# One product of tile 1 ahead of the second half of the k weights, and the norm of tile 4 ahead of the first statistics of tile 5

## The chip, the cores and the metric

The kernel runs on one core of one Trainium2 chip. It is written against the engines directly: TensorE (PE, with its weight loads shown as PEld), VectorE (DVE), ScalarE (ACT), GpSimd (POOL) and SyncE (SP, which here issues most DMAs). Each engine works through its own list of instructions in order, and semaphores hold an instruction until what it needs is done on another engine. The metric is the time of one execution on the device in microseconds (us); less is better.

## The reference

Two branches are added to the input x (2048 rows of 640): linear attention with 32 heads on the layer-normed x, and a block that selects 8 rows by a score, runs a gated MLP on them and adds the result back to these rows.

```python
xn = _layernorm(x)                                   # over the 640 columns
qkv = (xn @ wqkv).reshape(B, S, 3, H, Dh)            # q, k, v of 32 heads, 20 wide
phi = lambda t: jnp.where(t > 0, t + 1, jnp.exp(t)) + 1e-6
kv = einsum("bhsd,bhse->bhde", phi(k), v);  z = einsum("bhsd->bhd", phi(k))
o = einsum("bhqd,bhde->bhqe", phi(q), kv) / (einsum("bhqd,bhd->bhq", phi(q), z)[..., None] + 1e-6)
A = o @ wo
r = x @ w_r;  idx = argsort(-r)[:8]
y = (silu(x[idx] @ w_gate) * (x[idx] @ w_up)) @ w_down * sigmoid(r[idx])
out = x + A + (x + scatter of y to the rows idx)
```

## The kernel before

The 2048 rows are 16 tiles of 128. In the first third of the time each tile t goes through these steps, which the change concerns:

- the rows of x are loaded by DMA (issued by SP) into the second half of `XX`;
- statistics of the two halves of a row, `ln_a` (L155) and `ln_b` (L158), and their aggregate `ln_g` (L161), all on DVE;
- the scale 1/sqrt(variance) in `SR`, by a logarithm and an exponential on ACT: `ln_r` (L164, L165);
- the norm, `ln_xn` (L169) on DVE: `XX` first half = (x - mean) * SR;
- the transpose into `xnT`. Tiles 0 to 3 do it on PE (`tr_mm`, L178, in two parts of 2 and 3 column blocks of 128) and are copied out of PSUM by ACT or DVE (`tr_cp`, L185, L187). Tiles from 4 on do it by a DMA transpose that SP issues (`tr_dma`, L190);
- the k projection, `K` (L214) on PE: five products (kc = 0 to 4, the blocks of 128 columns) for each half h of the k columns, each half into one PSUM bank. The weights `wk` come in two DMAs, half 0 issued by ACT and half 1 by SP; `wk`'s half 0 is 320 columns, half 1 has one more, the routing score. `KA` is kc 0 and 1, `KB` is kc 2 to 4;
- phi(k): an exponential `PHe` (L233) and a relu `PHr` (L236) on ACT for each half, then `PHb` (L252) on DVE, which puts the tile's phi(k) into `pk`;
- `G` (L261, L268) on PE: the tile's normed rows times `pk`, summed over all tiles in PSUM banks 0 to 5.

After the last tile the matrix G, whose product with the v weights is the kv of the reference, is used for the rest: q projections (L489), denominators, the output matrix, the MLP of the chosen rows, and the output tiles (L761). The change does not touch these.

The order of every engine's work is written out by hand: the kernel is under a manual schedule, so the order of the calls in the text is the order on each engine, and waits are put where data demand them. Tiles 0 to 3 are interleaved call by call (L347 to L448); tiles 4 to 15 run in a loop (L449 to L479), where tile t's `K` stands ahead of `G(t - 1)`, `PHb(t - 1)` goes ahead of the norm of tile t + 2, and the statistics run three and four tiles ahead. PSUM banks 6 and 7 hold `K` of tiles 0, 2, 3 and up, banks 4 and 5 `K` of tile 1; banks 0 and 1 serve the PE transposes of tiles 0 and 2, banks 2 and 3 those of tiles 1 and 3, until `G` takes banks 0 to 5.

Around the first edit the PE order is: K(0) half 0; K(1) half 0, kc 0 and 1; K(0) half 1, kc 0 and 1; K(1) half 1, kc 0 and 1; K(0) half 1, the rest; transposes of tile 2 (2 blocks); K(1) half 1, the rest; transposes of tile 2 (3 blocks); K(1) half 0, the rest; K(2). The third and later blocks of tile 1 reach `xnT` by the copy `tr_cp(1, 1, 2, act)`. Around the second edit the DVE order is: `PHb(1)`, `ln_a(5)`, `ln_xn(4)`, `ln_b(5)`, `PHb(2)`, `ln_g(5)`, `ln_xn(5)`, `ln_a(6)`, `ln_b(6)`, `ln_g(6)`, `PHb(3)`.

Of the kernel before, what the change touches and what calls it, by code (L numbers as in the profile page):

```python
# [38 lines left out]
def kernel(  # L39
# [109 lines left out]
    def st_of(t):  # L149
        if t not in sts:  # L150
            sts[t] = tmp.tile([P, 2, nc.vector.BN_STATS_DIM], F32, tag="stats", name="stats", bufs=4)
        return sts[t]

    def ln_a(t):
        dve.bn_stats(out=st_of(t)[:, 0, :], in_=XX[:, t, 1, 0:320])  # L155
# [4 lines left out]
    def ln_g(t):  # L160
        dve.bn_aggr(out=MV[:, t, :], in_=sts[t][:])  # L161

    def ln_r(t):
        act.activation(lnv[:, t : t + 1], MV[:, t, 1:2], AF.Ln, bias=eps5[:])  # L164
        act.activation(SR[:, t : t + 1], lnv[:, t : t + 1], AF.Exp, scale=-0.5)  # L165

    def ln_xn(t, parts=((0, D),)):
        for a, b in parts:
            dve.tensor_scalar(out=XX[:, t, 0, a:b], in0=XX[:, t, 1, a:b], scalar1=MVf[:, t, 0:1],  # L169
                              scalar2=SR[:, t : t + 1], op0=ALU.subtract, op1=ALU.mult)  # L170
# [9 lines left out]
    def tr_cp(t, h, b0, eng):  # L180
        k0, k1 = TRP[h]
        src = PS[:, b0 + h, :].bitcast(BF16)[:, 0 : (k1 - k0) * P].rearrange("p (k c) -> p k c", c=P)
        dst = xnT[:, k0:k1, t * P : (t + 1) * P]
        if eng is act:
            act.copy(dst, src)  # L185
        else:
            dve.tensor_copy(dst, src)  # L187
# [17 lines left out]
    def off(t, h):  # L205
        return T - 1 - t if t != 1 and h else 0

    def K(t, hs=(0, 1), b=6, ks=range(KC)):
        for h in hs:
            if t > 4:  # L210
                pad(1)
            w = HW + h
            for kc in ks:
                pe.matmul(  # L214
                    PS[:, b + h, off(t, h) : off(t, h) + w],
                    lhsT=xnT[:, kc, t * P : (t + 1) * P],
                    rhs=wkh[h][:, kc, 0:w],
                    start=(kc == 0),
                    stop=(kc == KC - 1),
                )  # L220
# [3 lines left out]
    def phi_src(t, h, b):  # L224
        return PS[:, b + h, off(t, h) : off(t, h) + HW]

    def er(t):
        if t not in phis:
            phis[t] = tuple(tmp.tile([P, D], BF16, tag=k, name=k, bufs=3) for k in ("ek", "rk"))
        return phis[t]  # L230

    def PHe(t, h, b=6):
        act.activation(er(t)[0][:, h * HW : (h + 1) * HW], phi_src(t, h, b), AF.Exp)  # L233
# [20 lines left out]
    def pad(n):  # L254
        for _ in range(n):
            pe.ldweights(zero[:, 0:P])  # L256

    def G(t, ks=range(KC)):
        for a in ks:
            lhsT = XX[:, t, 0, a * P : (a + 1) * P]  # L260
            pe.matmul(  # L261
                PS[:, a, :], lhsT=lhsT, rhs=pk[:, t, 0:512],
                start=(t == 0), stop=(t == T - 1),
            )
            if t > 4:
                pad(2)
            if a < 4:
                pe.matmul(  # L268
                    PS[:, 5, a * P : (a + 1) * P], lhsT=lhsT, rhs=pk[:, t, 512:D],
                    start=(t == 0 and a == 0), stop=(t == T - 1), skip_group_check=True,  # L270
                )
# [74 lines left out]
    KA, KB = (range(0, 2), range(2, KC))  # L346
# [24 lines left out]
    tr_cp(1, 1, 2, act)  # L371
    ln_g(2)
    K(1, (0,), 4, KA)
    ln_r(2)
    K(0, (1,), 6, KA)
    PHe(0, 0, 6)
# [9 lines left out]
    tr_mm(2, 1, 0)  # L386
    ones(2)
    tr_cp(2, 0, 0, act)
    K(1, (0,), 4, KB)
    ln_g(3)  # L390
    PHr(0, 1, 6)
    tr_cp(2, 1, 0, dve)
# [30 lines left out]
    G(0, (3,))  # L423
    ln_r(4)
    K(3, (1,), 6, KB)
    ln_a(5)
    K(3, (0,), 6, KA)
    ln_xn(4)
    PHe(3, 1, 6)
    G(1)  # L430
    PHr(3, 1, 6)
# [531 lines left out]
```

## Time and profile before

| | |
|---|---|
| time, median of 3 runs | 106.49 us (106.16 to 106.72) |
| time of the profiled execution | 106.39 us |
| its span, first to last instruction | 104.7 us |
| granted TensorE clock, share of full speed | 0.999 |
| PE, DVE, ACT busy | 96%, 79%, 66% of the span |
| HBM read, written | 13.80 MB, 3.65 MB |

The span is what the profile shows between the first and the last instruction of the program; the time holds 1.7 us more around it. Times in the views are microseconds from the start of the span unless marked ns. Engines are named PE, PEld, DVE, ACT, POOL and SP; a q behind the name marks the sequencer that issues. L214 is line 214 of the kernel before. A matmul's end is modelled, so a busy PE is read by the distance of the starts of its products rather than by its share.

### The profile page before, as it was taken

How to read it: one execution, taken by the hardware profiler on the slowest of the kernel's cores; microseconds unless marked ns; L12 is line 12 of the kernel's file. 1: busy time of each engine (PE TensorE's matmuls, PEld its weight loads, DVE VectorE, ACT ScalarE, POOL GpSimd, SP SyncE). 2: the span in 40 equal slices, each digit the busy share in tenths (PEclk: the TensorE clock that was granted, in tenths of full speed). 3: DMA queues.
4: the chain of work that ended last, by engine and by line, in shares of the span. 5: the costliest groups of instructions: out<-in, count | busy, mean ns of one | idle time of the engine just before them, and what ended most of it. 6: DMA issues, size and time to landing. Idle time of an engine off the chain costs nothing.

```text
span 104.7 us, 2781 instructions
## 1 busy us (share of the span) xinstructions
PE 100.8 (96%) x924; PEld 72.8 (70%) x1148; DVE 82.8 (79%) x187; ACT 68.9 (66%) x171; POOL 16.3 (16%) x60
## 2 busy tenths in 40 slices
PE   6999999999999999999999999999999999999980
PEld 3357666668888888888777777875566767777760
DVE  1778989998888897873787867878988997888870
ACT  4288956766666666888599999886993997000000
POOL 7800000530000000000000025270000500000230
PEclk9999999999999999999999999999999999999999
DMA  2999914334756655899998999911460136895344
GB/s 57 299 347 379 282 38 87 74 66 86 146 134 80 152 122 125 179 267 346 241 391 275 343 332 377 348 51 39 160 228 9 30 101 202 192 364 185 130 129 125
DMA packets 23024, 19.67 MB, mean 188 GB/s; under 512 B 10594, under 2 KB 21474, under 8 KB 23010
## 3 DMA queue, kind: packets, MB, share of 16 engines
q1 hardware_dynamic: 21880, 19.01, 62.2%
q10 hardware_dynamic: 842, 0.46, 1.6%
q8 instruction: 8, 0.13, 0.6%
q0 software_dynamic: 288, 0.01, 0.3%
q14 instruction: 6, 0.05, 0.2%
HBM read 13.80 MB, written 3.65 MB: 167 GB/s over the span
## 4 chain that ended last, share of the span: by engine, by line
PE 89%; DMA 5%; SPq 1%; issue 1%; DVE 1%; DVEq 0%
PE PS L489 21%; PE PS L214 20%; PE PS L761 20%; PE PS L261 17%; DMA wk<-in_A_wqkv_dram 5%; PE PS L268 3%; PE PS L713 2%; PE PS L673 1%; SPq L103 1%; PE PS L555 1%; PE PS L737 1%; PE PS L684 1%; PE PS L282 1%; DVE o L774 1%; PE PS L635 1%
## 5 line engine op out<-in xcount | busy, mean ns | idle before, releaser
L214 PE MATMUL PS<-wk,xnT 128*128 128x320 bf16 (+1 forms) x160 | 25.0, 300 | 0.1
L261 PE MATMUL PS<-pk,XX 128*128 128x512 bf16 x80 | 23.7, 379 | 0.0
L489 PE MATMUL PS<-xnT,wq 128*128 128x512 bf16 x100 | 22.4, 379 | 0.0
L761 PE MATMUL PS<-Mb,pqT 128*128 128x320 bf16 (+4 forms) x165 | 22.1, 295 | 0.0
L256 PEld LDWEIGHTS <-zero 128*128 128x128 bf16 x224 | 18.2, 97 | 5.5
L233 ACT ACTIVATE ek<-PS 128x320 bf16<-128x320 f32 x32 | 14.0, 437 | 7.9 <-PE PS L214 7.9
L761 PEld LDWEIGHTS <-pqT 128*128 128x128 bf16 x165 | 15.8, 97 | 4.7 <-issue 0.3
L214 PEld LDWEIGHTS <-xnT 128*128 128x128 bf16 x160 | 15.2, 97 | 4.8 <-issue 0.3
L252 DVE SCALAR_TENSOR_TENSOR pk<-ek,rk 128x640 bf16<-128x640 bf16 x16 | 13.1, 817 | 4.1 <-ACT rk L236 3.9
L546 DVE SCALAR_TENSOR_TENSOR pqT<-qe,qr 128x512 bf16<-128x512 bf16 x20 | 13.6, 685 | 3.0 <-ACT qr L498 2.9
L497 ACT ACTIVATE qe<-PS 128x512 bf16<-128x512 f32 x20 | 12.3, 615 | 3.2 <-PE PS L489 3.2
L268 PE MATMUL PS<-pk,XX 128*128 128x128 bf16 x64 | 14.0, 219 | 0.0
L236 ACT ACTIVATE rk<-PS 128x320 bf16<-128x320 f32 x32 | 14.0, 436 | 0.0
L489 PEld LDWEIGHTS <-wq 128*128 128x128 bf16 x100 | 11.6, 118 | 2.9 <-issue 0.2
L498 ACT ACTIVATE qr<-PS 128x512 bf16<-128x512 f32 x20 | 12.3, 614 | 0.0
L770 DVE TENSOR_TENSOR o<-PS,XX 128x640 bf16<-128x640 f32 x11 | 9.0, 822 | 2.9 <-PE PS L761 2.0
L261 PEld LDWEIGHTS <-XX 128*128 128x128 bf16 x80 | 7.8, 98 | 4.2
L202 ACT ACTIVATE XX<-XX,MR,SR 128x640 bf16<-128x640 bf16 x11 | 9.4, 912 | 0.0
L155 DVE BATCH_NORM_STATS2 stats<-XX 128x6 f32<-128x320 bf16 x16 | 7.4, 463 | 1.9 <-DMA XX<-in_A_x_dram 1.9
L169 DVE TENSOR_SCALAR XX<-XX,MVf,SR 128x640 bf16<-128x640 bf16 (+2 forms) x17 | 7.3, 437 | 1.3 <-ACT SR L165 1.3
L158 DVE BATCH_NORM_STATS2 stats<-XX 128x6 f32<-128x320 bf16 x16 | 7.7, 479 | 0.0
L274 POOL MEMSET XX<- 128x1 bf16 x18 | 1.9, 112 | 35.2 <-DMA xnT<-XX 21.0
(114 smaller groups left out, 101.2 us busy)
## 6 DMA issues: line engine op xcount, KB each, us to landing
out_dram<-o SPq DMA_DIRECT2D x15, 160.0 KB, 2.0
XX<-in_A_x_dram SPq DMA_DIRECT2D x3, 640.0 KB, 7.9
wg<-in_B_w_gate_dram SPq DMA_DIRECT2D x5, 384.0 KB, 8.8
wu<-in_B_w_up_dram SPq DMA_DIRECT2D x5, 384.0 KB, 6.1
wd<-in_B_w_down_dram SPq DMA_DIRECT2D x1, 1920.0 KB, 11.3
wv<-in_A_wqkv_dram SPq DMA_DIRECT2D x5, 160.0 KB, 3.5
wq<-in_A_wqkv_dram SPq DMA_DIRECT2D x1, 800.0 KB, 6.2
hi_d<-XX SPq DMA_DIRECT2D x1, 800.0 KB, 3.9
```

What stands on the lines that cost most here:

```text
L214: pe.matmul(PS[:, b + h, off(t, h) : off(t, h) + w], lhsT=xnT[:, kc, t * P : (t + 1) * P], rhs=wkh[h][:, kc, 0:w], start=(kc == 0), stop=( ...
L233: act.activation(er(t)[0][:, h * HW : (h + 1) * HW], phi_src(t, h, b), AF.Exp)
L236: act.activation(er(t)[1][:, h * HW : (h + 1) * HW], phi_src(t, h, b), AF.Relu)
L252: dve.scalar_tensor_tensor(out=pk[:, t, :], in0=ek[:], scalar=1.0, in1=rk[:], op0=ALU.min, op1=ALU.add)
L256: pe.ldweights(zero[:, 0:P])
L261: pe.matmul(PS[:, a, :], lhsT=lhsT, rhs=pk[:, t, 0:512], start=(t == 0), stop=(t == T - 1),)
L268: pe.matmul(PS[:, 5, a * P : (a + 1) * P], lhsT=lhsT, rhs=pk[:, t, 512:D], start=(t == 0 and a == 0), stop=(t == T - 1), skip_group_check= ...
L489: pe.matmul(PS[:, bank, :], lhsT=by5(wq[:, kc, :])[:, m, :], rhs=xnT[:, kc, tb * TBLK : (tb + 1) * TBLK], start=(kc == 0), stop=(kc == KC ...
L497: act.activation(e, PS[:, bank, :], AF.Exp)
L498: act.activation(r, PS[:, bank, :], AF.Relu)
L546: dve.scalar_tensor_tensor(out=pqT[:, m, tb * TBLK : (tb + 1) * TBLK], in0=e, scalar=1.0, in1=r, op0=ALU.min, op1=ALU.add,)
L761: pe.matmul(PS[:, b, o : o + c1 - c0], lhsT=pqT[:, kc, t * P : (t + 1) * P], rhs=Mb[:, kc, c0:c1], start=(kc == 0), stop=(kc == KC - 1))
```

## The change

Two calls change their place. Of the three products that `K(1, (0,), 4, KB)` issued in one go (kc 2, 3, 4 of tile 1 against half 0 of the k weights), the one for kc = 2 now stands right behind the products for kc 0 and 1, ahead of the first product on half 1 of the weights; kc 3 and 4 stay where they were. And on DVE the norm of tile 4 now stands ahead of the first statistics of tile 5. No instruction is added or removed.

```diff
     ln_g(2)
     K(1, (0,), 4, KA)
+    K(1, (0,), 4, (2,))
     ln_r(2)
     K(0, (1,), 6, KA)
     PHe(0, 0, 6)
...
     tr_cp(2, 0, 0, act)
-    K(1, (0,), 4, KB)
+    K(1, (0,), 4, (3, 4))
     ln_g(3)
...
     G(0, (3,))
     ln_r(4)
     K(3, (1,), 6, KB)
-    ln_a(5)
     K(3, (0,), 6, KA)
     ln_xn(4)
+    ln_a(5)
     PHe(3, 1, 6)
     G(1)
```

## The prediction

> **What bounds the kernel now.** I read the page first, then the chain of waits, then busy time by stage.
>
> ```profile
> span 104.7 us, 2781 instructions
> PE 100.8 (96%) x924; PEld 72.8 (70%) x1148; DVE 82.8 (79%) x187; ACT 68.9 (66%) x171; POOL 16.3 (16%) x60
> ...
> PE 89%; DMA 5%; SPq 1%; issue 1%; DVE 1%; DVEq 0%
> ```
> ```profile
> 2.20 5.50 DMA wk<-in_A_wqkv_dram
> ```
> ```profile
> 8.90:13.45 4.55, 4.55 (x41) 3.15 (x39) 4.37 (x12) 4.49 (x16) 0.20 (x2) 1.00 1.03 296
> ```
> ```profile
> 7.75:101.00 93.25, 93.25 (x891) 69.14 (x1115) 77.31 (x168) 64.65 (x160) 11.89 (x41) 1.00 0.65 186
> ```
>
> The chain runs through the DMA of the second half of the k weights (issued 2.20, landed 2.20 + 5.50 = 7.70) and from there almost wholly through TensorE (its 89%). In the two rows by stage the columns are stretch, its length, busy PE, PEld, DVE, ACT, POOL, granted clock, DMA share and GB/s. PE fills all of the 93.25 from 7.75 to 101 at a clock of 1.00. So nothing after 7.75 can soak up lost PE time: what PE loses there, the end loses, and what it gains has to be let through by every later wait. ACT is as full as PE from 8.90 to 13.45 (4.49 of 4.55), where the change lies; DVE is nearly so. The change moves hundredths of a microsecond, so the waits must be read one by one.
>
> **Part 1, the moved product.** Rows of the timeline, each from a narrow window of its own and put in order of time: start, length, engine, line, operation; a row with a count is a run of equal instructions, and brackets tell how long the engine stood before it and for whom.
>
> ```profile
> 6.35 0.15 PEld L214 LDWEIGHTS <-xnT 128*128 128x128 bf16 x2
> 6.41 0.30 PE L214 MATMUL PS<-wk,xnT 128*128 128x320 bf16 x1
> 7.04 0.48 ACT L185 COPY xnT<-PS 128x384 bf16<-128x384 bf16 x1
> 7.12 0.57 PE L214 MATMUL PS<-wk,xnT 128*128 128x320 bf16 x3
> 7.75 0.10 PEld L214 LDWEIGHTS <-xnT 128*128 128x128 bf16 x1 [0.26 <-issue]
> 9.24 0.37 ACT L185 COPY xnT<-PS 128x256 bf16<-128x256 bf16 x1
> 9.53 0.43 PE L214 MATMUL PS<-wk,xnT 128*128 128x320 bf16 x2
> 9.66 0.10 PEld L214 LDWEIGHTS <-xnT 128*128 128x128 bf16 x1
> 11.48 0.47 DVE L158 BATCH_NORM_STATS2 stats<-XX 128x6 f32<-128x320 bf16 x1
> 11.87 0.27 DVE L187 COPY xnT<-PS 128x256 bf16<-128x256 bf16 x1
> 11.98 0.59 PE L261 MATMUL PS<-pk,XX 128*128 128x512 bf16 x2
> ```
>
> The pace of these products is (0.57 - 0.30) / 2 = 0.135 us. The last one ahead of the weights starts at 7.12 + 2 x 0.135 = 7.39, so the next could start at 7.525; it starts at 7.75. That hole of 0.225 takes the moved product, if its own operand is there: columns 2 to 4 of tile 1, copied by ACT until 7.04 + 0.48 = 7.52. A wait hands over in about 0.04 (ACT's end at 15.83 to DVE's start at 15.87, rows in part 2), so its weights load from 7.56. From the start of a load to its product is 6.41 - 6.35 = 0.06: product at 7.62, next at 7.62 + 0.135 = 7.755 against 7.75. The row does not show this load behind a wait followed by one more load, so I bound the lag by 0.06 and by the load's full 0.10: the next product is 0.005 to 0.045 late; I take 0.01, since the 0.06 is a row of the same line. [...]
>
> What is removed is one of the three products of tile 1 that end at 9.53 + 2 x 0.135 = 9.80, thus 0.135. It is not all let through. The first load of tile 2 waits for the copy that ends at 9.24 + 0.37 = 9.61; with the handover that is 9.65, and it stands at 9.66 now. So the load cannot move; its product, at 9.80 now, can start at 9.65 + 0.06 = 9.71, a gain of 0.09. Next, G of tile 0 into bank 2 needs the copy of tile 3 out of that bank: 11.87 + 0.27 = 12.14, handed over by 12.18. In the row of two products the second ends at 11.98 + 0.59 = 12.57 and lasts 0.38 (the 512-wide ones), so it starts at 12.19 now. And that copy stands on DVE right behind the second statistics of tile 4 (11.48 + 0.40 = 11.88), so an earlier PE does not pull it forward. Of 0.135 there is 0.01 to 0.02 left after 12.2. Bounds: -0.135 (all kept) to nothing; I take -0.01, since both waits have rows. ACT is not moved either, being full up to 13.45 and started off by the products on the second half; it only shares their 0.01.
>
> **Part 2, the norm of tile 4 ahead of the first statistics of tile 5.** Rows of DVE, with those of ACT and PE that they meet, chosen in the same way:
>
> ```profile
> 12.46 0.81 DVE L252 SCALAR_TENSOR_TENSOR pk<-ek,rk 128x640 bf16<-128x640 bf16 x1
> 13.19 0.49 DVE L155 BATCH_NORM_STATS2 stats<-XX 128x6 f32<-128x320 bf16 x1
> 13.25 0.20 ACT L165 ACTIVATE SR<-lnv 128x1 f32<-128x1 f32 x1
> 13.59 0.43 DVE L169 TENSOR_SCALAR XX<-XX,MVf,SR 128x640 bf16<-128x640 bf16 x1
> 13.94 0.48 DVE L158 BATCH_NORM_STATS2 stats<-XX 128x6 f32<-128x320 bf16 x1
> 14.34 0.80 DVE L252 SCALAR_TENSOR_TENSOR pk<-ek,rk 128x640 bf16<-128x640 bf16 x1
> 15.07 0.20 DVE L161 BATCH_NORM_AGGREGATE MVf<-stats 128x2 bf16<-128x12 f32 x1
> 15.41 0.38 PE L261 MATMUL PS<-pk,XX 128*128 128x512 bf16 x1
> 15.63 0.20 ACT L165 ACTIVATE SR<-lnv 128x1 f32<-128x1 f32 x1
> 15.87 0.45 DVE L169 TENSOR_SCALAR XX<-XX,MVf,SR 128x640 bf16<-128x640 bf16 x1 [0.60 <-ACT SR L165]
> 16.23 0.49 DVE L155 BATCH_NORM_STATS2 stats<-XX 128x6 f32<-128x320 bf16 x1
> 16.69 0.12 PEld L214 LDWEIGHTS <-xnT 128*128 128x128 bf16 x2 [0.15 <-DMA xnT<-XX]
> 17.27 0.77 DVE L252 SCALAR_TENSOR_TENSOR pk<-ek,rk 128x640 bf16<-128x640 bf16 x1
> 18.09 0.38 PE L261 MATMUL PS<-pk,XX 128*128 128x512 bf16 x1
> ```
>
> The norm needs the scale that ACT finishes at 13.25 + 0.20 = 13.45. In the old order the statistics of tile 5 run from 13.19 and cover that wait; the norm follows at 13.59. In the new order DVE is free for the norm at 13.19 and must stand until 13.45 + 0.04 = 13.49 (the same handover: 15.83 to 15.87). The norm, and with it the transpose DMA of tile 4, gains 0.10; everything behind it on DVE pays. The statistics follow a norm by 0.36 (15.87 to 16.23), so they start at 13.85; the second statistics by 0.40 (13.19 to 13.59), at 14.25 against 13.94; pk of tile 2 at 14.65 against 14.34. All of that is 0.31 late.
>
> First customer: G of tile 2 at 15.41 needs pk of tile 2. That ended at 14.34 + 0.80 = 15.14; now 15.45, handed over at 15.49: PE stands 0.08. This also uses up the 0.01 of part 1. Second customer: the aggregate of tile 5 (15.07 to 15.38), its two ACT steps, its norm. In the old trace DVE waits 0.60 there for ACT, but that wait is a round trip that starts from the aggregate, so it hides nothing: the norm goes from 15.87 to 16.18, the statistics of tile 6 from 16.23 to 16.54, pk of tile 3 from 17.27 to 17.58, its end from 18.04 to 18.35. Third customer: G of tile 3 stands at 18.09, which is 0.05 behind the end of pk of tile 3; it has no slack. It goes to 18.40, 0.31 late. The 0.08 from G of tile 2 lies inside this and is not added. The earlier transpose of tile 4 is worth nothing: its product at 16.69 waits for it by a hair now, but PE arrives there 0.08 later anyway.
>
> From there PE and DVE are both 0.31 late, side by side, and no later stretch has room.
>
> **The transposes behind it.** SP issues the one of tile 5 when the norm of tile 5 ends, 0.31 later:
>
> ```profile
> 16.34 1.58 SPq L190 DMA_TRANSPOSE xnT<-XX  x1
> 19.22 0.27 PEld L214 LDWEIGHTS <-xnT 128*128 128x128 bf16 x2
> 22.07 0.11 PEld L214 LDWEIGHTS <-xnT 128*128 128x128 bf16 x2
> ```
> ```profile
> DMA to landing us min/median/max: 2.6/2.7/3.3
> ```
> ```profile
> DMA to landing us min/median/max: 2.7/2.7/2.7
> ```
> ```profile
> DMA to landing us min/median/max: 3.2/3.2/3.2
> ```
>
> The three landing rows are from the view of the transposes' line (L190): nine of them together, tile 5 alone, tile 6 alone. Issued at 16.65 and landed 2.7 later that is 19.35; the load that waits for it stood at 19.22 and would come at 19.53. Covered by 0.14 (after the handover). If it took the 3.2 of tile 6 it would land at 19.85 and cost 19.89 - 19.53 = 0.36 more. Between 2.6 and 3.3 I take its own 2.7, cost nothing. Tile 6 (load at 22.07) shifts with PE.
>
> **Sum**, against the profiled execution's own 106.39 (span 104.7): 0.01 late at the weights, which ACT and then DVE carry along, + 0.31 at G of tile 3; the 0.01 left of the product is lost in the stand at G of tile 2. 106.39 + 0.32 = 106.71. The median of the runs is 106.49, 0.10 above that execution; on it the sum would be 106.81. I forecast 106.75, between them, +0.25% on the median.
>
> **The rivals.** (a) Not slower, the head start kept because DVE's hole never reaches PE: what is in favour is a real hole of 0.225 and a transpose that PE waits for at 16.69. It needs pk of tile 3 to end by 18.05, thus a DVE delay of zero, thus the scale of tile 4 ready by 13.15 in place of 13.45. Against it: ACT is full up to there. Then the gain lies between 0.01 and 0.135: 106.26 to 106.38, on the median 106.36 to 106.48. (b) Clearly slower: the transpose of tile 5 lands late. For it: one of its neighbours took 3.2, and it decides from 2.84 us on (19.53 - 0.04 - 16.65). Against it: tile 5 took 2.7 itself, and the median of nine is 2.7. Price 0.32 + 0.36: 107.07, on the median 107.17. (c) The moved product doesn't fit into the hole. Where the weights land at 7.5 or before, it stands in front of the work on them: without it that work starts at 7.53, with it at 7.755, and ACT and DVE go along, 0.22 late. The price is then 0.32 + 0.22 = 0.54: 106.93. For it: the landing is the only thing here that no engine sets. Against it: in this execution the weights landed 0.18 behind the copy, at 7.70. (d) The change doesn't do what it says, because DVE's order makes no difference to G of tile 3: then part 1 alone is left, 106.38, the weak end of (a), whose chance it shares.
>
> **How the numbers follow.** Forecast 0.58, (a) with (d) 0.14, (b) 0.20, (c) 0.08. The range takes in the low end of (a), 106.26, and (b) on the median, 107.17, to within 0.02: 106.25 to 107.15, with the forecast's own between 106.55 and 106.95. By 0.5% (0.53 us, about what a measurement of this kernel can tell from no change): slower gets all of (b) and half of (c), whose 0.54 lies on the bound, and 0.07 of the forecast, for terms mis-sized by 0.2: 0.31. Faster gets half of (a), 0.07: even its full 0.135 is a quarter of the bound, so this is room for a gain that no row shows. The same: the rest, 0.62.
>
> **What would show it.** In the changed kernel: a product at about 7.6 in the hole, the first product on the second half still at 7.75 to 7.80; a hole of about 0.3 on DVE ahead of the norm of tile 4, released by ACT; pk of tile 2 and 3 ending near 15.45 and 18.35; PE standing some 0.08 ahead of G of tile 2 and 0.2 ahead of G of tile 3. Wrong would be: no hole on DVE there, or G of tile 3 at or before 18.1, or the loads of tile 5 released by the DMA.

## The result, and the profile after

The changed kernel takes 106.88 us (median of 22 runs, 106.65 to 107.47), the kernel before 106.56 in the same comparison. The ratio is 1.0035, with a 95% interval of 1.0020 to 1.0051: slower by about a third of a percent, inside the half percent that was called no change, and 0.13 above the forecast of 106.75. The difference of the two medians is 0.32.

The page of the changed kernel:

```profile
span 105.0 us, 2773 instructions
PE 100.0 (95%) x916; PEld 72.5 (69%) x1148; DVE 82.6 (79%) x187; ACT 68.8 (66%) x171; POOL 16.3 (16%) x60
...
PE 89%; DVE 3%; DMA 2%; issue 1%; DVEq 0%
```

Eight of PE's 924 products have no record here (the change removes none), so a single gap of 0.22 on PE with no releaser is a missing row and not a wait. The span is 0.3 longer. The DMA of the k weights, 5% of the chain before, is gone from the chain. That is the first thing to look at: why? The timeline around the moved product, chosen rows, and then the row of the half-1 load in the table of DMA issues (the last number is the time from issue to landing), of the kernel before and of the changed one:

```profile
6.66 0.90 ACT L185 COPY xnT<-PS 128x256 bf16<-128x256 bf16 x2
7.61 0.11 PEld L214 LDWEIGHTS <-xnT 128*128 128x128 bf16 x2 [0.22 <-ACT xnT L185]
7.62 0.45 PE L214 MATMUL PS<-wk,xnT 128*128 128x320 bf16 x2
```
```profile
wk<-in_A_wqkv_dram SPq DMA_DIRECT2D x1, 400.0 KB, 5.5
```
```profile
wk<-in_A_wqkv_dram SPq DMA_DIRECT2D x1, 400.0 KB, 5.3
```

In this execution the weights landed at 2.20 + 5.3 = 7.50, before the copy that the moved product waits for was done (6.66 + 0.90 = 7.56). The product starts at 7.62, and the first product on half 1, the second of that row, at 7.76. Without the moved product it could have started at 7.56, one pace of 0.135 behind the product at 7.42. So the hole of 0.225 that the trace of before showed was not there, and the moved product made one of its own, 0.06 of standing for the copy.

The second part, in the order in which it unrolls (chosen rows):

```profile
12.42 0.82 DVE L252 SCALAR_TENSOR_TENSOR pk<-ek,rk 128x640 bf16<-128x640 bf16 x1
13.26 0.20 ACT L165 ACTIVATE SR<-lnv 128x1 f32<-128x1 f32 x1
13.49 0.45 DVE L169 TENSOR_SCALAR XX<-XX,MVf,SR 128x640 bf16<-128x640 bf16 x1 [0.26 <-ACT SR L165]
13.86 0.49 DVE L155 BATCH_NORM_STATS2 stats<-XX 128x6 f32<-128x320 bf16 x1
13.97 1.20 SPq L190 DMA_TRANSPOSE xnT<-XX  x1
14.65 0.81 DVE L252 SCALAR_TENSOR_TENSOR pk<-ek,rk 128x640 bf16<-128x640 bf16 x1
15.52 0.38 PE L261 MATMUL PS<-pk,XX 128*128 128x512 bf16 x1
16.18 0.45 DVE L169 TENSOR_SCALAR XX<-XX,MVf,SR 128x640 bf16<-128x640 bf16 x1 [0.60 <-ACT SR L165]
16.66 1.48 SPq L190 DMA_TRANSPOSE xnT<-XX  x1
16.85 0.30 PE L214 MATMUL PS<-wk,xnT 128*128 128x320 bf16 x1
17.58 0.77 DVE L252 SCALAR_TENSOR_TENSOR pk<-ek,rk 128x640 bf16<-128x640 bf16 x1
18.41 0.38 PE L261 MATMUL PS<-pk,XX 128*128 128x512 bf16 x1
19.53 0.27 PEld L214 LDWEIGHTS <-xnT 128*128 128x128 bf16 x2
```

The bracket behind the norm at 13.49 is the new hole on DVE, released by ACT's scale. From it all of DVE runs late: pk of tile 2 by 0.31 (14.34 to 14.65), the norm of tile 5 by 0.31, pk of tile 3 by 0.31 (17.27 to 17.58). PE pays at G of tile 3: 18.09 before, 18.41 now. The transpose of tile 4 is issued 0.08 earlier (14.05 to 13.97), which brings nothing: PE reaches that tile's products at 16.85, 0.14 later than before.

### The profile page after: what moved, and what is told of

The parts are those of the page before. It is cut to its first block, busy times and chain, and to the rows that moved or that the text cites. A ratio compares the mean times of both kernels' runs of the same rounds, so it can differ in the third digit from the quotient of the medians.

```text
span 105.0 us, 2773 instructions
## 1 busy us (share of the span) xinstructions
PE 100.0 (95%) x916; PEld 72.5 (69%) x1148; DVE 82.6 (79%) x187; ACT 68.8 (66%) x171; POOL 16.3 (16%) x60
## 4 chain that ended last, share of the span: by engine, by line
PE 89%; DVE 3%; DMA 2%; issue 1%; DVEq 0%
PE PS L214 21%; PE PS L490 21%; PE PS L762 20%; PE PS L261 16%; PE PS L268 4%; DMA XX<-in_A_x_dram 2%; PE PS L714 2%; PE PS L674 1%; PE PS L556 1%; PE PS L178 1%; PE PS L738 1%; PE PS L685 1%; PE PS L282 1%; DVE stats L155 1%; DVE XX L169 1%
## 5 line engine op out<-in xcount | busy, mean ns | idle before, releaser
L261 PE MATMUL PS<-pk,XX 128*128 128x512 bf16 x75 | 22.7, 379 | 0.0
```

The lines of the kernel that those rows point to most:

```text
L261: pe.matmul(PS[:, a, :], lhsT=lhsT, rhs=pk[:, t, 0:512], start=(t == 0), stop=(t == T - 1),)
```

## The experiments

Each kernel was timed against the kernel before on the same chip; kernels sent together share its runs. The number to follow in the traces is the distance from the first product on half 1 of the k weights to the first product of G of tile 3. It leaves out what happens ahead of the first point, which differs from execution to execution. "Rest" is the profiled execution's time less the first point. Both starts are read from the timeline.

| kernel | half 1 (or its first part) landed | first product on it | G of tile 3 | distance | profiled time | rest |
|---|---|---|---|---|---|---|
| before | 7.71 | 7.75 | 18.09 | 10.34 | 106.39 | 98.64 |
| changed | 7.50 | 7.76 | 18.41 | 10.65 | 106.76 | 99.00 |
| changed, again | 7.44 | 8.08 | 18.73 | 10.65 | 107.02 | 98.94 |
| product alone | 7.19 | 7.71 | 18.04 | 10.33 | 106.34 | 98.63 |
| norm alone | 7.21 | 7.50 | 18.17 | 10.67 | 106.53 | 99.03 |
| norm alone, again | 7.79 | 7.92 | 18.56 | 10.64 | 106.88 | 98.96 |
| changed, hole filled | 7.88 | 7.92 | 18.24 | 10.32 | 106.54 | 98.62 |
| norm, hole filled | 7.73 | 8.00 | 18.38 | 10.38 | 106.72 | 98.72 |
| DVE delayed | 7.67 | 7.71 | 18.42 | 10.71 | 106.83 | 99.12 |
| split load | 6.66 | 7.52 | 17.88 | 10.36 | 106.47 | 98.95 |
| split, product | 6.62 | 7.87 | 18.20 | 10.33 | 106.77 | 98.90 |
| split, norm | 6.71 | 7.47 | 18.11 | 10.64 | 106.69 | 99.22 |
| split, both | 6.56 | 7.81 | 18.46 | 10.65 | 107.03 | 99.22 |
| split, x loads merged | 6.31 | 7.59 | 17.96 | 10.37 | 106.26 | 98.67 |

**The moved product alone.**

```diff
     K(1, (0,), 4, KA)
+    K(1, (0,), 4, (2,))
...
-    K(1, (0,), 4, KB)
+    K(1, (0,), 4, (3, 4))
```

> The moved product alone, DVE's order as before. My theory: the product's 0.135 us is not let through; G of tile 0 into bank 2 still starts at about 12.2 and G of tile 3 at about 18.1, so the ratio to the kernel before lies between 1.000 (weights of half 1 landing at 7.7, where the product fits into the hole) and 1.002 (weights landing at 7.5, where it stands ahead of their work). Rival, the head start is kept: G of tile 3 at about 17.95, ratio 0.9987.

106.65 us, ratio 1.0007 (0.9991 to 1.0024). The first product of G of tile 3:

```profile
18.04 0.38 PE L261 MATMUL PS<-pk,XX 128*128 128x512 bf16 x1
```

That is 10.33 behind the first product on half 1, against 10.34: of the 0.135 taken out of the later work at most 0.01 is left, as the two waits of the prediction had it. The weights had landed at 7.19 here and their work still started only at 7.71, for PE first stood for the copy that the moved product needs, and then did that product:

```profile
7.56 0.11 PEld L214 LDWEIGHTS <-xnT 128*128 128x128 bf16 x2 [0.22 <-ACT xnT L185]
```

**The norm's move alone**, twice.

```diff
-    ln_a(5)
     K(3, (0,), 6, KA)
     ln_xn(4)
+    ln_a(5)
```

> The norm of tile 4 ahead of the first statistics of tile 5, alone. My theory: DVE stands about 0.3 us ahead of the norm, pk of tile 3 ends 0.31 later, G of tile 3 starts at about 18.4; ratio 1.003. Rival, the order on DVE is free and the difference comes from the moved product: ratio 1.000, G of tile 3 at about 18.1. Rival, the earlier transpose of tile 4 pays: ratio 0.999.

> The norm's move alone, once more, since its first time (0.12 us above the kernel before) fell short of the 0.31 that its trace showed and of the 0.35 that it cost beside the split load. My theory: the first time was drawn from executions whose weights landed early; now 0.25 to 0.35 above, ratio 1.002 to 1.0035. Rival, without the moved product about two thirds of it are taken back: 0.12 again, ratio 1.001.

First time 106.65 us, ratio 1.0007 (0.9990 to 1.0024); second time 106.67, ratio 1.0012 (0.9990 to 1.0033). The traces show the expected wait and the expected distance in both (10.67 and 10.64); the rows of the first:

```profile
13.25 0.45 DVE L169 TENSOR_SCALAR XX<-XX,MVf,SR 128x640 bf16<-128x640 bf16 x1 [0.20 <-ACT SR L165]
```
```profile
18.17 0.38 PE L261 MATMUL PS<-pk,XX 128*128 128x512 bf16 x1
```

The time agrees less well: 0.31 us would be a ratio of 1.0029, which is inside the second interval and outside the first. The repeated expectation was missed. See the open point below.

**The hole filled, by an earlier scale.** In the changed kernel, ACT does the scale of tile 4 ahead of the relu of tile 2's half 0, and the two products of tile 3 that write that relu's bank go behind G of tile 1, so that they don't wait for it.

```diff
+    ln_r(4)
     PHr(2, 0, 6)
     G(0, (3,))
-    ln_r(4)
     K(3, (1,), 6, KB)
-    K(3, (0,), 6, KA)
     ln_xn(4)
     ln_a(5)
     PHe(3, 1, 6)
     G(1)
+    K(3, (0,), 6, KA)
```

> The changed kernel, with the scale of tile 4 brought up on ACT ahead of the relu of tile 2's half 0, and the two products that reuse that bank moved behind G of tile 1. My theory, it is the lateness of ACT's scale that makes DVE stand: the scale is ready at about 13.13, DVE has no hole ahead of the norm, pk of tile 3 ends at about 18.05 and G of tile 3 starts at about 18.1; ratio to the kernel before 1.000 to 1.002 (what the moved product costs at the weights). Rival, having the statistics behind the norm is itself what costs (the order, not the wait): G of tile 3 stays at about 18.4, ratio 1.003 or more.

106.55 us, ratio 0.9996 (0.9981 to 1.0012). ACT's scale, DVE's norm and G of tile 3:

```profile
13.09 0.20 ACT L165 ACTIVATE SR<-lnv 128x1 f32<-128x1 f32 x1
```
```profile
13.33 0.45 DVE L169 TENSOR_SCALAR XX<-XX,MVf,SR 128x640 bf16<-128x640 bf16 x1
```
```profile
18.24 0.38 PE L261 MATMUL PS<-pk,XX 128*128 128x512 bf16 x1
```

The norm still stands ahead of the statistics, but its bracket is gone: the scale ends at 13.29, and the norm starts at 13.33, as soon as pk of tile 1 lets it. G of tile 3 comes 10.32 behind the first product on half 1. With the order of the change on DVE and without the wait the 0.31 are gone; it was the wait and not that order. (This kernel also moves two products on PE, so it is not a test of the wait by itself; the delayed DVE below tests it from the other side.)

**The same without the moved product.** The diff is the last one on top of the norm's move alone.

> The norm's move with the scale of tile 4 brought up on ACT and the two products behind G of tile 1, without the moved product. My theory: DVE has no hole ahead of the norm, G of tile 3 follows the first product on half 1 by 10.3 as in the kernel before, in place of 10.66; ratio 0.999 to 1.001, thus 0.3 faster than the norm's move alone. Rival, the order costs without the wait: 1.003.

106.72 us, ratio 1.0013 (0.9993 to 1.0033). The distance is 10.38, as in the kernel before, against 10.64 of the norm's move on the same chip. In the time it is not faster than that move (106.67). So the trace bears out the expectation, and the timed runs miss it: 0.3 faster was expected.

**DVE delayed, with the old order.**

```diff
     ln_xn(4)
+    dve.memset(spare[:], 0.0)
     PHe(3, 1, 6)
```

> The kernel before, order unchanged, with a memset of 128x640 (about 0.3 us on DVE) behind the norm of tile 4, so that the transpose of tile 4 keeps its time and only pk of tile 2, the norm of tile 5 and pk of tile 3 come later. My theory: G of tile 3 has no slack and starts about 0.3 later, at 18.4; ratio 1.003, as in the changed kernel. Rival, the loss comes through another road than DVE's lateness: G of tile 3 at about 18.1, ratio 1.000.

106.84 us, ratio 1.0027 (1.0005 to 1.0048). The memset, and G of tile 3 (line numbers are one higher in this kernel, for the line that makes `spare`):

```profile
14.08 0.33 DVE L430 MEMSET spare<- 128x320 uint32 x1
```
```profile
18.42 0.38 PE L262 MATMUL PS<-pk,XX 128*128 128x512 bf16 x1
```

The distance is 10.71, the rest 99.12. Lateness of DVE behind the norm of tile 4, put in by itself, costs about what the change costs and at the same place: 0.37 in the distance, for a memset of 0.33. No later stretch takes it back in this trace.

**The load of half 1 split**, so that the weights of blocks 0 and 1 are always there in time, and on top of it the product, the norm's move and both.

```diff
-    ld(sp, wkh[1][:, :, 0:HW], wqkv_v[:, :, D + HW : 2 * D])
+    ld(sp, wkh[1][:, 0:2, 0:HW], wqkv_v[:, 0:2, D + HW : 2 * D])
+    ld(sp, wkh[1][:, 2:KC, 0:HW], wqkv_v[:, 2:KC, D + HW : 2 * D])
```

> The kernel before with the load of the second half of the k weights cut in two (blocks 0 and 1, then 2 to 4), so that the first products on it no longer wait for the whole. In the profiles so far that load landed between 7.19 and 7.88, and the first product on it started at the later of about 7.53 and the landing. My theory: it now starts at about 7.53 always; G of tile 3 follows 10.34 behind it, at about 17.87; the time loses its spread and ratio is 0.998 to 0.999. Rival, the extra issue on SP delays the loads of x behind it and eats this: ratio 1.000 or more.

> The split load and the moved product. My theory: with the weights always there, the product only stands in front of their work: first product on half 1 at about 7.72 in place of 7.53, later distance to G of tile 3 shorter by 0.05 (10.29); 0.10 to 0.15 us slower than the split load alone. Rival, the product is free or helps even so: equal to the split load alone, or faster by 0.1.

> The split load and the norm of tile 4 ahead of the first statistics of tile 5. My theory: G of tile 3 follows the first product on half 1 by 10.66 in place of 10.34; 0.32 us slower than the split load alone. Rival, as the time of the norm alone hinted (0.12 above the kernel before): a part of it is taken back behind G of tile 3, so 0.1 slower than the split load alone.

> The split load and both parts of the change. My theory: first product on half 1 at about 7.72, G of tile 3 at about 18.38; 0.45 to 0.5 us slower than the split load alone, the sum of the two. Rival, the two parts cover each other: slower than the split load alone by no more than the norm's part.

| | time | ratio to before |
|---|---|---|
| split | 106.63 | 1.0018 (1.0001 to 1.0035) |
| split, product | 106.67 | 1.0022 (1.0004 to 1.0040) |
| split, norm | 106.98 | 1.0059 (1.0036 to 1.0082) |
| split, both | 107.07 | 1.0067 (1.0044 to 1.0090) |

On this common ground the norm's move costs 106.98 - 106.63 = 0.35 and both parts 0.44. The product costs 0.04 to 0.09 by the medians, less than the 0.10 to 0.15 expected, and its distance is 10.33, not the 10.29 expected. The traces show more than the medians: the first product on half 1 starts at 7.87 and 7.81 with it, 7.52 and 7.47 without it, though the weights had landed by 6.71 in all four. Of that, 0.15 lies ahead of the change, since the first k product, too, starts at 6.54 and 6.50 with it, 6.39 and 6.35 without it. From the first k product on it is 1.33 and 1.31 against 1.13 and 1.12: the product costs 0.20 there.

The split load itself was to make the kernel faster and made it slower. The rival's reason, late loads of x, is not what the trace shows. All of DVE, ACT and PE run about 0.2 earlier than in the kernel before, to their last instructions. The loss is at the very end. The waits of SP on the last line of the program, from 102 us on, in the kernel before and in this one:

```profile
SPq L958 <- DMA out_dram<-o: 0.5, 2, 0.3
```
```profile
SPq L959 <- DMA out_dram<-o: 1.1, 1, 1.1
```

There SP asks the DMA semaphores one after the other, in the order of its list, about 0.06 us each (in the trace of the kernel before, the first three start 0.06 and 0.07 apart). The kernel before waits twice for up to 0.3 us, on the last outputs as they land, and the last to land is asked last. In this kernel, with one DMA more, the last output's semaphore stands near the front of that order: SP stands on it for 1.1 us, until 103.55, and then asks five more until 103.9, where the kernel before is at 103.8 with its work done 0.2 later.

**The split load with the count of DMAs restored.**

```diff
-    for a, b in ((4, 8), (8, 12), (12, 16)):
+    for a, b in ((4, 8), (8, 16)):
         ld(sp, XX[:, a:b, 1, :], x_v[:, a:b, :])
```

> The kernel before with the split load of half 1, and the loads of x tiles 8 to 11 and 12 to 15 made one, so that the number of DMAs, and with it the order of the DMA semaphores, is that of the kernel before. In the split load's trace all engines run 0.2 earlier up to the end and lose it in the last waits, where SP asks the semaphores one by one and the last output's now comes second in place of last. My theory: the loss goes, the gain stays: 0.15 to 0.25 us faster than the kernel before in a trace with late weights, ratio 0.9975 to 0.999. Rival, the loss at the end has another cause: ratio 1.001 to 1.002 as with the split load alone.

106.30 us against 106.55, ratio 0.9981 (0.9959 to 1.0003). The rest is 98.67, that of the kernel before within 0.03; with the split alone it was 98.95. So the place of the last output in the final waits was worth 0.28. The same row as above:

```profile
SPq L959 <- DMA out_dram<-o: 0.5, 2, 0.3
```

This is the fastest kernel of the study. It beats the changed one clearly (106.30 to 106.94 on the same chip) and the kernel before by 0.25, where the interval just reaches 1. The merged load of x without the split was not run, so how much of the 0.25 the split alone brings is not shown.

**The changed kernel again**, beside these.

> The changed kernel once more, beside the norm's move alone on the same chip. My theory: ratio 1.003 to 1.004 to the kernel before; against the norm's move alone it adds what the moved product costs where the weights land early, 0.05 to 0.15 us. Rival, the moved product costs nothing: equal to the norm's move alone.

106.94 us, ratio 1.0037 (1.0016 to 1.0058), 0.27 above the norm's move alone on the same chip, more than the 0.05 to 0.15 expected.

## Why the prediction was right

**The bound.** PE without a pause from 7.75 on, so that what it loses the end loses: borne out. In every trace of the table the rest follows the distance (98.6 to 98.7 where it is 10.3 to 10.4, 98.9 to 99.1 where it is 10.6 to 10.7), apart from the four with the split load and the x loads as before: their rest is 0.2 to 0.3 longer, which the split load's own trace shows in the final waits.

**Part 1, gain.** The two waits that were to swallow the head start did: tile 2's first product at 9.68 waits for ACT's copy, and G of tile 0 into bank 2 starts at 12.22 against 12.20. The product alone leaves the distance at 10.33. That gain was put at 0.01 and is 0.01.

**Part 1, price.** Here the term was right for some executions only. The sum took the landing of the weights at 7.70 from one execution and gave the case that they come earlier, rival (c), a chance of 0.08. In the nine traces with the unsplit load the landing runs from 7.19 to 7.88, and in four of them it is at 7.50 or below. What the product costs is read from the first k product on (6.44 in the changed kernel), because that start differs between executions too. Where the weights of half 1 are not the last to come, the first product on them starts 1.11 to 1.13 behind the first k product in the six traces without the moved product, and 1.31 to 1.33 behind it in four with it (1.54 in the changed kernel again, where the first two products took 0.23 longer). So the moved product costs 0.20 there: its own 0.135 and some 0.06 of standing for the copy. Rival (c) had 0.22. Where the weights are the last to come, the product costs nothing: their work starts 0.04 behind the landing with it (landed 7.88, start 7.92, the changed kernel with the hole filled) as without it (7.71 and 7.75, the kernel before). In the medians of timed runs it is worth 0.04 to 0.27, according to the pair.

The 106.93 of rival (c) is a slip of the prediction: it adds the price for early weights to an execution in which they came late. With early weights the kernel before would by that reckoning itself be 0.22 faster, so the changed kernel comes out at 106.71 either way, and only its distance to the kernel before differs.

The profile of the changed kernel is such a case, so it was partly luck that it has the first product at 7.76 and a time of 106.76 as forecast: there was no hole to fill. Two small errors also cancel. The copy was done 0.04 later than assumed, and the lag from load to product, put at 0.06, hardly shows: load and product start at 7.61 and 7.62, and the next product 0.15 behind the load, against a pace of 0.135.

**The number.** The measured difference of the medians, 0.32, is the 0.32 of the sum. The result lies 0.13 above the forecast because the kernel before came out at 106.56 this time and not at 106.49 (0.07), and because the forecast stood 0.06 below the sum on the median (106.81). That the difference is met to a hundredth is luck as well: part 1 costs nothing or 0.20 according to the landing, and the norm's move alone, which was to bring the 0.31, brought less in the timed runs (see the open point).

**Part 2.** Every term came out within 0.03: scale done 13.45 (13.46), norm 13.49 (13.49), pk of tile 2 14.65 (14.65), G of tile 2 15.49 (15.52), norm of tile 5 16.18 (16.18), pk of tile 3 ending 18.35 (18.35), G of tile 3 18.40 (18.41). The hole filled and the memset show the cause from both sides: take the wait away and keep the order, and the loss goes; keep the order of before and add the lateness, and the loss comes. One wait was not named: the first product of tile 4 comes at 16.85, 0.25 behind the product ahead of it where the kernel before has 0.22, right behind the end of the relu of tile 3 on ACT (16.80), itself 0.31 late; this lies inside the 0.31.

**The rivals.** (a), the head start kept: out, by the distance of the product alone. (b), tile 5's transpose late: it was issued at 16.66 and landed 2.6 later, at about 19.27, some 0.26 ahead of the load at 19.53; not in this trace. (c), the moved product in front of early weights: borne out in part, see the price above. (d), DVE's order without effect: out.

**What stays open.** The norm's move alone cost 0.12 to 0.17 by the medians, in two series, where its traces show 0.30 to 0.33 in the distance, and where it cost 0.35 beside the split load. In its two profiled executions nothing is given back behind G of tile 3: the rest is 99.03 and 98.96, against 98.64 of the kernel before. Up to the norm its instructions are those of the kernel before, so the starts of its executions should be drawn alike. Whether the timed runs had earlier starts by chance, or whether something gives back a part in executions that were not profiled, these runs do not settle. So the 0.31 is shown in the traces, and in the timed runs its size is uncertain.

## What to carry to other kernels

Here the norm moved ahead on DVE, which works in order, was paid for with the wait in front of it: DVE stood 0.26 there, and pk of tile 2 came 0.31 later. So look up when the input of a moved operation is ready, and whether what used to stand in between was covering that wait. Then follow the lateness to the next consumer without slack; here that was four operations and 5 us away. The hole of 0.225 that waited for a DMA in the trace of before was not there in every execution: the load landed between 7.19 and 7.88, in four traces of nine at 7.50 or below. Look at several landings before something is put into such a hole, or make the transfer earlier instead. Here the earlier transfer, together with the restored number of DMAs, was 0.25 faster by the medians, with an interval that just reaches no change, where the change lost 0.3.

## What the runs showed of the hardware

The place of the last DMA's semaphore in the waits at the end of the program was worth 0.28 us here (rest 98.95 with the split load, 98.67 with the number of DMAs restored). One DMA more near the start had moved it (one wait of 1.1 on the outputs there), and one less moved it back (two waits, 0.5 together).

The same 400 KB load, issued at 2.20 in all nine traces in which it is not split, landed between 7.19 and 7.88. Ahead of it the start varies for other reasons too. In the norm's move repeated PE waits for half 0:

```profile
6.81 0.43 PE L214 MATMUL PS<-wk,xnT 128*128 128x320 bf16 x2 [0.40 <-DMA wk<-in_A_wqkv_dram]
```

And in the changed kernel repeated the first two products take 0.66 where the first profile of the same kernel has 0.43:

```profile
6.54 0.66 PE L214 MATMUL PS<-wk,xnT 128*128 128x320 bf16 x2
```
```profile
6.44 0.43 PE L214 MATMUL PS<-wk,xnT 128*128 128x320 bf16 x2
```

The warm-up products of PE ahead of them differ more. They start at 3.79 in the kernel before and at 3.78 in the two profiles of the changed kernel, and last 1.91, 1.13 and 2.08 us; the changed kernel again, and its first profile:

```profile
3.78 2.08 PE L121 MATMUL PS<-const-float32-0.0 128*128 128x512 f32 x2
```
```profile
3.78 1.13 PE L121 MATMUL PS<-const-float32-0.0 128*128 128x512 f32 x2
```

The granted clock reads 1.00 in both from 4 to 8, so these rows do not show why the two last differently.
